# Decay attention with a routed MLP: the scores of two heads as one fp32 product each, straight from the raw rows

## The chip, the cores and the metric

The kernel runs on one core of one Trainium2 chip. The core has TensorE (PE, matrix products and transposes into PSUM), VectorE (DVE), ScalarE (ACT), GpSimd (POOL), SyncE (SP, which here only issues DMAs) and 16 DMA engines. The metric is the device time of one execution in microseconds.

## The reference

```python
# q, k, v: (8, 8, 576, 64); f: (8, 8, 576); w1: 512 x 1024, w2: 1024 x 512, capacity 128
scores = matmul(q, k.T) / sqrt(64)
cum = cumsum(log(clip(f, 1e-4, 1)))
scores = where(causal, -1e9, scores + cum[:, None] - cum[None, :])
attn = exp(scores - max(scores)); attn /= sum(attn) + 1e-9
x = matmul(attn, v)                      # all heads side by side: 576 x 512 per batch
score = x @ w_gate                       # per token
top = the 128 tokens with the largest score
y = relu(x[top] @ w1) @ w2
out = x; out[top] = x[top] + sigmoid(score[top]) * y
```

## The kernel before

The 64 heads are taken as 32 pairs, the two heads of a pair on the two halves of the 128 partitions (64 values of a head each). Of the 576 positions, the first 64 (R) make a short block and the rest four blocks of 128.

For a pair, `pair_ops` loads the raw rows of k (tile `rk`, two DMAs) and of q (tile `rq`, four DMAs into the block layout, with zeros where the short block's product of both heads needs them). Then it splits each into a rounded high part and the rest: `kh`, `qh` by a copy in the type fp32r (L469, POOL), `kl`, `ql` by a subtraction (L476, POOL, for the first 14 pairs also DVE). It also loads, for each head, the row of decays `e` broadcast to all partitions (L500), and has POOL cut it into masked pieces `m` (L370 `affine_select`).

`pair_parts` then makes the scores in six units (rows i, columns k0 to k1): five units of 192 to 448 columns with one product per head on each half of the rows of PE, and one full-height unit of 64 columns for the short block of both heads (`units`, L515 on). Each unit is three products in fp32r, high by high, high by low and low by high (`sc`, L587), two records each for the two heads. DVE adds the decay and takes the minimum (L611, a custom operation that reads the scores in PSUM and `e` or `m`), ACT takes the exponential with a sum (L671), PE transposes the result (`tp`, L691 to L701), ACT or DVE copies it out (`pt`, L308 or L312), PE multiplies by v (`av`, L765; fp32, the two heads on the two halves of the columns of PE), and the result is transposed back (`tb`, L821) and divided by the sums (L827). Per batch a gate is summed (POOL L842, DVE L846), tokens are ranked and the 128 best gathered, and the MLP runs on PE in three fp32r products per tile (L1109 to L1170) with weights that `weight_part` splits during the first half of the run (high L901, low L904).

What is issued in what order is worked out beforehand in Python by the class `Flow`: each piece of work is added with a cost per engine that may take it, what it waits for, a place and the slots (buffers) that it takes and gives back. `Flow.run` goes through a model of the engines' clocks and issues the work in that order; each engine keeps this order. Buffers: two raw k tiles, two raw q tiles, a ring of two for the rounded tiles, two `e`, two `m` per head parity, one tile `x` for half a batch's outputs, eight PSUM banks. `GAP` is the planner's time for a switch of PE from one kind of work to another.

Of the kernel before, what the change touches and what calls it, by code (L numbers as in the profile page):

```python
# [8 lines left out]
F32 = mybir.dt.float32  # L9
# [8 lines left out]
P = 128  # L18
# [12 lines left out]
class Flow:  # L31
# [7 lines left out]

    LAG = {"pe": 0.2, "act": 0.17, "dve": 0.12, "pool": 0.17, "sp": 0.05}  # L40
# [5 lines left out]
           ("turn", "long"): -0.08, ("turn", "short"): -0.08,  # L46
# [41 lines left out]
    def run(self, issued):  # L88
        left = self.todo
        while left:  # L90
# [22 lines left out]
            self.clock[e] = s + t["cost"][e]  # L113
# [22 lines left out]
def kernel(  # L136
# [33 lines left out]
    BD = 0.511  # L170
    WP = 17
    WQ = 3
    R0 = 1.186
    X0 = -3.065
    XE_ = -16.604
    XH_ = 4.193
    XM_ = -24.434
    XB_ = 3.482
    XN_ = -3.264
    XO_ = -0.662  # L180
    XU_ = 0.399
    XQ_ = -1.504
    XR_ = 4.546
    XG_ = 4.106
    PL4 = 42.349
    GW = 175.03
    EPS = 0.011
    LOOK = 13
    HELP1 = 0
    HELP2 = 14  # L190
    SPLIT = 14
    PR = -23.786
    PL = -11.67
    PS = -11.252
    PV = -37.418
    PM = -4.974
    PE_ = 22.794
    PC = -5.754
    PB = 8.281
    PD = 14.978  # L200
    VO = -3.496
    VD = 1
    GD = 0.1
    WS = 29.806
    WD = 12.682
    WL = -15.905
    RK = 30.632
    RD = 8.583
    XP = 0.323
    GO = 12.534  # L210
    GS = 1.969
    GL = 8.861
# [3 lines left out]
    SP = -18.988  # L216
# [10 lines left out]
    def bank(nm):  # L227
# [12 lines left out]
    RING = 2  # L240
# [9 lines left out]
    es = [const.tile([P, S], F32, name=f"e{r}") for r in range(2)]  # L250
    ms = [const.tile([P, 2 * FR + 320 + 448], F32, name=f"m{r}") for r in range(2)]
# [41 lines left out]
    def row(n, k=1):  # L293

        return {"pe": k * max(n * 0.0004375 + 0.0105, 0.108)}
# [18 lines left out]
    flow = Flow({"ps": 8, "raw": 2, "rq": 2, "v": 3, "p0": 4, "p1": 4, "p4": 2, "pt": 2, "ot": 2,  # L314
                 "x": 1, "nm": 10, "h": 1, "hth": 1, "htl": 1, "xth": 1, "xtl": 1, "xe": 2, "srow": 1,
# [120 lines left out]
    raws, ops, used = {}, {}, {}  # L436
# [3 lines left out]
    def pair_ops(p):  # L440
        pl = 9 * p - PL
        r = p % RING
        qh, ql, kh, kl = (ts[r] for ts in (qhs, qls, khs, kls))
        old = used.get(p - RING, [])
        tk = {"q": Token("rq", 2), "k": Token("raw", 2)}
# [9 lines left out]
        def t_q(e):  # L455

            t = raws["q", p] = rqs[p % 2]
# [8 lines left out]
        def hi(dst, nm):  # L466
            def fn(e):
                if e == "pool":
                    nc.gpsimd.tensor_scalar(dst, raws[nm, p], 1.0, 0.0, ALU.mult, ALU.add)  # L469
                else:  # L470
                    copy_on(e, dst, raws[nm, p])
            return fn

        def lo(dst, hi_, nm):
            def fn(e):
                (nc.vector if e == "dve" else nc.gpsimd).tensor_tensor(dst, raws[nm, p], hi_.bitcast(F32), ALU.subtract)  # L476
            return fn

        c1 = {"pool": 0.64}
        c2 = {"pool": 1.46}  # L480
        if p < HELP1:
            c1 = {"pool": 0.64, "act": 0.55, "dve": 0.68}
        if p < HELP2:
            c2 = {"pool": 1.46, "dve": 1.15}
        pl = 9 * p - PS
# [5 lines left out]
        used[p] = []  # L491

        for hh in range(2):
            h = 2 * p + hh
            e_, m_ = es[h % 2], ms[h % 2]
            olde, oldm = decused.get(("e", h - 2), []), decused.get(("m", h - 2), [])
# [42 lines left out]
    def pair_parts(p):  # L539
# [21 lines left out]
        for u, (i, k0, k1) in enumerate(units):  # L561
# [20 lines left out]
            def sc(e, ls, rs, first, last, u=u, i=i, k0=k0, k1=k1):  # L582
                r = p % RING
                for hh in range(2 if i < NF else 1):
                    rows = slice(hh * D, hh * D + D) if i < NF else slice(0, P)
                    o = st["sc", u][hh][:, 0:k1 - k0]
                    nc.tensor.matmul(o, q_rows(ls[r], rows, i), rs[r][rows, k0:k1], start=first, stop=last)  # L587
# [30 lines left out]
            c = row(n)["pe"] if i < NF else pr(n)["pe"]  # L618
            kd = "row" if i < NF else "short"
            if p < SPLIT:  # L620
# [3 lines left out]
            else:  # L624
                x2 = add({"pe": 3 * c}, lambda e, s0=s0, s1=s1, s2=s2: (s0(e), s1(e), s2(e)),
                         after=ops[p][0] + ops[p][1] + ahead, place=place, take=tk_b + tk_n, kind=kd)
            scored[i] = x2
            used[p].append(x2)
            for hh in range(2 if i < NF else 1):
                h = 2 * p + hh  # L630
                def e_(n_, h=h):
                    return lambda: es[h % 2][:, 0:n_]

                def m_(a, b_, h=h, i=i):
                    o_ = {0: 0, 1: 2 * FR, 2: 2 * FR + 320}[i]
                    return lambda: ms[h % 2][:, o_ + a:o_ + b_]

                def m3(h=h):
                    f_ = ms[h % 2][:, FR + P:FR + P + 1]
                    return bass.AP(f_.tensor, f_.offset, [f_.ap[0], [-R, 3], [1, R]])  # L640
# [241 lines left out]
    def weight_part(n):  # L882
# [20 lines left out]
        x2 = add({**({"dve": w / 500 + 0.1} if n < WP else {}), **({"pool": w / 424 + 0.08} if n >= WQ else {})},  # L903
# [355 lines left out]
```

## Time and profile before

| | us |
|---|---|
| median of 3 runs | 448.5 |
| lowest and highest run | 446.15, 450.13 |
| the profiled execution, its own time | 451.17 |
| its span, first to last instruction | 449.4 |

| engine | busy us | share of the span |
|---|---|---|
| PE | 425.1 | 95% |
| DVE | 346.5 | 77% |
| ACT | 338.0 | 75% |
| POOL | 334.9 | 75% |

How to read the rows: L587 is line 587 of the kernel. A name such as sc<-kh,qh is the tile that is written and those that are read. A PE record's busy time reaches from its start until its result is out; records that follow each other overlap, so the time that one costs is the distance from its start to the next start. An fp32 product stands in the profile as two records, an fp32r product and a transpose as one. "x33" counts records. "Idle before <- " is the time for which the engine had nothing in hand before the group, and what ended it. PEclk is the granted clock of PE, as a share of 2.4 GHz.

### The profile page before, as it was taken

To read this page: it belongs to the slowest core of one execution; us is meant where nothing else is said; L and a number is where in the kernel's file an instruction comes from. 1 tells how busy PE (TensorE), PEld (TensorE's weight loads), DVE (VectorE), ACT (ScalarE), POOL (GpSimd) and SP (SyncE) were. 2 spreads that over 40 slices of the span, in tenths; PEclk is the share of its full clock that TensorE was granted. 3 is DMA by queue.
4 is the path that set the end of the run, shared out by engine and by line. 5 is a ranking of instruction groups with operands and counts; after the bars stand their busy time and mean duration, and the time that the engine had idled before them with its cause. 6 is when DMAs were issued, how large, how long until landed. Compare 5 with 4: busy or idle time off the path is not lost. (4 is left out here: it accounts for less than half of the span.)

```text
span 449.4 us, 11669 instructions
## 1 busy us (share of the span) xinstructions
PE 425.1 (95%) x3329; PEld 325.2 (72%) x3329; DVE 346.5 (77%) x1514; ACT 338.0 (75%) x1091; POOL 334.9 (75%) x511
## 2 busy tenths in 40 slices
PE   2999996999989999999999999999999999999995
PEld 1677766686858677868678686868686877878784
DVE  5478988789998689878968987779949995967531
ACT  3479995799988899988789896979987797913221
POOL 7879997799798889987969688689839794142100
PEclk9999996999998999999999999999999999999999
DMA  6566784667766757475554626465546432121010
GB/s 156 155 196 212 195 254 126 195 165 223 195 202 177 217 144 204 118 206 164 187 157 144 202 85 193 159 174 183 159 131 184 135 107 81 54 77 48 23 48 23
DMA packets 73286, 68.07 MB, mean 151 GB/s; under 512 B 25700, under 2 KB 57479, under 8 KB 73223
## 3 DMA queue, kind: packets, MB, share of 16 engines
q1 hardware_dynamic: 71862, 62.99, 47.9%
q0 software_dynamic: 1280, 4.20, 2.8%
q8 instruction: 27, 0.44, 0.4%
q14 instruction: 37, 0.30, 0.3%
q10 hardware_dynamic: 80, 0.15, 0.1%
HBM read 55.59 MB, written 11.70 MB: 150 GB/s over the span
## 5 line engine op out<-in xcount | busy, mean ns | idle before, releaser
L671 ACT ACTIVATE p<-p,nm 128x192 f32<-128x192 f32 (+4 forms) x288 | 166.4, 582 | 19.1 <-DVE nm L611 18.6
L308 ACT COPY pt<-tp 64x128 f32<-64x128 f32 (+4 forms) x386 | 123.9, 365 | 21.0 <-PE tp L696 12.5
L370 POOL TENSOR_SCALAR_AFFINE_SELECT m<-e 128x320 f32<-128x320 f32 (+3 forms) x256 | 111.9, 463 | 25.7 <-DMA e<-eq 15.7
L696 PE MATMUL tp<-ident,p 128*128 128x128 f32 x640 | 112.2, 290 | 6.5 <-DVE nm L611 4.3
L611 DVE CUSTOM_DVE_ANT_0 p<-sc,m 128x320 f32<-128x320 f32 (+3 forms) x224 | 90.0, 429 | 19.4 <-PE sc L587 14.8
L696 PEld LDWEIGHTS tp<-ident,p 128*128 128x128 f32 x640 | 79.2, 147 | 26.5 <-DVE nm L611 6.3
L765 PE MATMUL av<-pt,v 128*64 128x448 f32 (+4 forms) x768 | 91.1, 391 | 0.8 <-DVE nm L611 0.8
L765 PEld LDWEIGHTS av<-pt,v 128*64 128x64 f32 x768 | 45.6, 137 | 42.2 <-issue 29.1
L842 POOL TENSOR_TENSOR gj<-x,wg 128x512 f32<-128x512 f32 x64 | 56.0, 887 | 24.6 <-DVE x L827 20.1
L587 PE MATMUL sc<-kh,qh 64*128 64x192 f32 (+4 forms) x352 | 71.6, 356 | 2.8 <-DVE nm L611 1.7
L587 PE MATMUL sc<-kl,qh 64*128 64x192 f32 (+4 forms) x352 | 64.5, 319 | 0.0
L587 PE MATMUL sc<-kh,ql 64*128 64x192 f32 (+4 forms) x352 | 63.2, 315 | 0.5 <-DVE ql L476 0.5
L587 PEld LDWEIGHTS sc<-kh,qh 64*128 64x128 f32 (+1 forms) x352 | 40.7, 192 | 20.6 <-issue 5.5
L671 ACT ACTIVATION_READ_ACCUMULATOR p<-p,nm 128x1 f32 x288 | 55.2, 192 | 0.0
L476 POOL TENSOR_TENSOR kl<-rk,kh 128x576 fp32r<-128x576 f32 x32 | 46.6, 1456 | 0.2
L611 DVE CUSTOM_DVE_ANT_0 p<-sc,e 128x384 f32<-128x384 f32 x64 | 33.9, 553 | 14.3 <-PE sc L587 12.9
L993 DVE TENSOR_SCALAR_CACHE_REDUCE j<-srow,sg 128x384 uint8<-128x384 f32 (+6 forms) x72 | 41.0, 570 | 1.6
L587 PEld LDWEIGHTS sc<-kh,ql 64*128 64x128 f32 (+1 forms) x352 | 40.6, 194 | 1.1 <-DVE ql L476 0.7
L587 PEld LDWEIGHTS sc<-kl,qh 64*128 64x128 f32 (+1 forms) x352 | 40.0, 194 | 1.0 <-issue 0.5
L476 POOL TENSOR_TENSOR ql<-rq,qh 128x640 fp32r<-128x640 f32 x25 | 38.9, 1554 | 0.2
L308 ACT COPY ot<-av 128x128 f32<-128x128 f32 (+1 forms) x62 | 21.8, 399 | 22.4 <-PE av L765 18.6
L1181 POOL DMA_INDIRECT out_dram<-xe,idx x8 | 8.2, 1031 | 35.8 <-DVE xe L1177 23.2
(108 smaller groups left out, 754.3 us busy)
## 6 DMA issues: line engine op xcount, KB each, us to landing
e<-eq SPq DMA_DIRECT2D x62, 288.0 KB
rq<-in_qk_dram SPq DMA_DIRECT2D x64, 128.0 KB
out_dram<-x SPq DMA_DIRECT2D x16, 512.0 KB
rk<-in_qk_dram SPq DMA_DIRECT2D x32, 192.0 KB
v<-in_v_dram SPq DMA_DIRECT2D x32, 192.0 KB
rk<-in_qk_dram SPq DMA_DIRECT2D x32, 96.0 KB
srow<-sd SPq DMA_DIRECT2D x7, 320.0 KB
v<-in_v_dram SPq DMA_DIRECT2D x32, 64.0 KB
```

Of the source, the lines that this page charges most:

```text
L308: nc.scalar.copy(d, s_)
L370: nc.gpsimd.affine_select(out=dst, in_=src, pattern=w, compare_op=ALU.is_ge, fill=NEG, base=base, channel_multiplier=1)
L476: (nc.vector if e == "dve" else nc.gpsimd).tensor_tensor(dst, raws[nm, p], hi_.bitcast(F32), ALU.subtract)
L587: nc.tensor.matmul(o, q_rows(ls[r], rows, i), rs[r][rows, k0:k1], start=first, stop=last)
L611: nc.vector.tensor_tensor_reduce(out=part(hh, i)[:, x0 - o:x1 - o], in0=b_[:, x0 - k0:x1 - k0], in1=in1(), scale=-0.125, scalar=BIG if fir ...
L671: nc.scalar.activation(x, x, AF.Exp, bias=st["nm", hh, i], scale=-1.0, accum_out=l)
L696: nc.tensor.transpose(tp[:, pos:pos + P], t_[:, o:o + P], ident)
L765: nc.tensor.matmul(avb[p, g][par * D:(par + 1) * D, qo + q0 - g * SPL:qo + q1 - g * SPL], vt[:, j, par * D:(par + 1) * D], pt[:, off:off + ...
L842: nc.gpsimd.tensor_tensor(out=gj[0:n, c0:c1, :], in0=xhs[key][0:n, c0:c1, w0:w1], in1=wg[0:n, hb * HB + w0:hb * HB + w1].unsqueeze(1).broa ...
L993: nc.vector.tensor_scalar(junk[0:n, 0:w, :], src, sg()[0:n, c:c + 1], None, op, ALU.add, accum_out=cnt[0:n, k, c:c + 1])
L1181: nc.gpsimd.indirect_dma_start(out=outs[b][:, :], out_offset=bass.IndirectOffsetOnAxis(ap=q["idx"][0:nr, 0:1], axis=0), in_=q["xe"][0:nr, ...
```

## The change

The scores are one fp32 product per head and unit, directly from the raw tiles `rq` and `rk`. The tiles of the rounded and low parts and the copies and subtractions that fill them go. Raw k, raw q, `e` and `m` get a third tile, `x` a second one. A raw tile is given back by the last of the pair's six score units instead of by the subtraction. The planner's cost for a score unit becomes four passes per column at 2400 columns per us plus 0.03, PE's costs count double before 22 us, some switch times change, and about 50 place constants take new values. The weights' low parts are now open to POOL for all tiles.

```diff
+    HALF = 22.0
-           ("turn", "long"): -0.08, ("turn", "short"): -0.08,
+           ("turn", "long"): 0.01, ("turn", "short"): 0.02, ("long", "turn"): 0.02, ("short", "turn"): 0.02,
...
-            self.clock[e] = s + t["cost"][e]
+            self.clock[e] = s + t["cost"][e] * (2 if e == "pe" and s < self.HALF else 1)
...
-    WQ = 3
+    WQ = 0
...
-    rawp = ctx.enter_context(tc.tile_pool(name="rawp", bufs=2))
+    rawp = ctx.enter_context(tc.tile_pool(name="rawp", bufs=3))
...
-    qhs, qls, khs, kls = ([const.tile([P, w], F32R, name=f"{nm}_{r}") for r in range(RING)]
-                          for nm, w in (("qh", QW), ("ql", QW), ("kh", S), ("kl", S)))
-    rqs = [const.tile([P, QW], F32, name=f"rq{r}") for r in range(2)]
-    es = [const.tile([P, S], F32, name=f"e{r}") for r in range(2)]
-    ms = [const.tile([P, 2 * FR + 320 + 448], F32, name=f"m{r}") for r in range(2)]
+    RQ = 3
+    rqs = [const.tile([P, QW], F32, name=f"rq{r}") for r in range(RQ)]
+    es = [const.tile([P, S], F32, name=f"e{r}") for r in range(3)]
+    ms = [const.tile([P, 2 * FR + 320 + 448], F32, name=f"m{r}") for r in range(3)]
...
-    def row(n, k=1):
-        return {"pe": k * max(n * 0.0004375 + 0.0105, 0.108)}
+    def row(n):
+        return {"pe": n * 4 / 2400 + 0.03}
...
-        tk = {"q": Token("rq", 2), "k": Token("raw", 2)}
+        tk = tks[p] = {"q": Token("rq", 6), "k": Token("raw", 6)}
...
-        a0 = add(c1, hi(kh, "k"), after=[lk] + old, place=pl, give=[tk["k"]])
-        a1 = add(c1, hi(qh, "q"), after=[lq] + old, place=pl + 0.01, give=[tk["q"]])
-        a2 = add(c2, lo(kl, kh, "k"), after=[a0] + old, place=pl + 0.02, give=[tk["k"]])
-        a3 = add(c2, lo(ql, qh, "q"), after=[a1] + old, place=pl + 0.03, give=[tk["q"]])
-        ops[p] = ([a0, a1], [a2, a3])
+        ops[p] = [lk, lq]
...
-            def s1(e, sc=sc):
-                sc(e, qhs, khs, True, False)
-            def s2(e, sc=sc):
-                sc(e, qhs, kls, False, False)
-                sc(e, qls, khs, False, True)
+                    nc.tensor.matmul(st["sc", u][hh][:, 0:k1 - k0], q_rows(raws["q", p], rows, i), raws["k", p][rows, k0:k1],
+                                     start=True, stop=True)
...
-                x1 = add({"pe": c}, lambda e, s0=s0, s1=s1: (s0(e), s1(e)), after=ops[p][0] + ahead, place=place,
-                         take=tk_b + tk_n, kind=kd)
-                x2 = add({"pe": 2 * c}, s2, after=ops[p][1] + [x1], place=place + 0.05, kind=kd)
+            x2 = add(row(n) if i < NF else {"pe": 0.23}, lambda e, s0=s0, sc=sc: (s0(e), sc(e)), after=ops[p] + ahead, place=place,
+                     take=tk_b + tk_n, give=list(tks[p].values()), kind="row" if i < NF else "short")
...
-                xhs[key] = work.tile([P, NCH, HB], F32, tag="x", name=f"x{b}_{hb}", bufs=1)
+                xhs[key] = work.tile([P, NCH, HB], F32, tag="x", name=f"x{b}_{hb}", bufs=2)
```

## Rows read from the trace of the kernel before

**Rows 1.** Busy time of each engine (records in brackets) in four stretches.
```profile
0.00:28.60 28.60, 20.08 (x87) 15.18 (x87) 14.68 (x58) 13.09 (x32) 22.78 (x58) 1.00 0.58 158
28.60:160.94 132.34, 123.00 (x1057) 93.31 (x1056) 112.19 (x462) 115.85 (x391) 117.97 (x173) 0.96 0.68 198
160.94:379.00 218.06, 216.87 (x1799) 166.66 (x1798) 178.91 (x844) 185.50 (x607) 178.95 (x264) 1.00 0.53 156
379.00:449.40 70.40, 65.11 (x394) 50.06 (x390) 40.67 (x152) 23.52 (x61) 15.18 (x18) 0.99 0.13 47
```

Columns of rows 1: the stretch and its length; PE, PE's weight loads, DVE, ACT, POOL; PEclk; DMA share; GB/s.

**Rows 2.** The same view for tiles tp, tb, sc, av alone; PE first.
```profile
28.60:160.94 132.34, 45.68 (x305) 36.16 (x304) 5.79 (x15) 44.57 (x144) 0.96 0.68 198
...
28.60:160.94 132.34, 7.86 (x55) 5.98 (x55) 9.36 (x20) 0.96 0.68 198
...
28.60:160.94 132.34, 44.86 (x402) 35.11 (x402) 58.90 (x159) 0.96 0.68 198
...
28.60:160.94 132.34, 34.41 (x288) 17.01 (x288) 0.61 (x1) 7.83 (x23) 0.96 0.68 198
```

**Rows 3.** Timeline of PE, a pair's scores: start us, us, line, operation.
```profile
334.73 0.28 PE L587 MATMUL sc<-kh,qh 128*128 128x64 f32 x1
...
335.16 0.36 PE L587 MATMUL sc<-kh,qh 64*128 64x192 f32 x2
...
337.09 0.36 PE L587 MATMUL sc<-kl,qh 64*128 64x448 f32 x2
337.30 0.37 PE L587 MATMUL sc<-kh,ql 64*128 64x448 f32 x2
337.59 0.44 PE L696 MATMUL tp<-ident,p 128*128 128x128 f32 x2
```

**Rows 4.** Timeline of PE, short windows from 102.3 to 106.3: av, then transposes.
```profile
102.32 0.60 PE L765 MATMUL av<-pt,v 128*64 128x448 f32 x2
...
102.74 0.55 PE L765 MATMUL av<-pt,v 128*64 128x448 f32 x2
...
103.12 0.55 PE L765 MATMUL av<-pt,v 128*64 128x448 f32 x2
...
105.17 0.66 PE L696 MATMUL tp<-ident,p 128*128 128x128 f32 x4
...
106.23 0.28 PE L587 MATMUL sc<-kh,qh 128*128 128x64 f32 x1
```

**Rows 5.** Timeline of PE near 9.5 us: broadcast of the decay rows.
```profile
9.28 0.68 PE L426 MATMUL eb<-ec,ident 64*128 64x288 f32 x1
...
9.76 0.68 PE L426 MATMUL eb<-ec,ident 64*128 64x288 f32 x1
```

**Rows 6.** Instructions of L904 and L476 on DVE: ns min/median/max, starts.
```profile
L904 DVE TENSOR_TENSOR w1l<-wst,w1h x4: 1391/2002/5645, 31.9 to 65.1; 128x1024 fp32r<-128x1024 f32 x4
...
L476 DVE TENSOR_TENSOR ql<-rq,qh x7: 826/1011/3055, 9.4 to 137.2; 128x640 fp32r<-128x640 f32 x7
```

**Rows 7.** Timeline from 65 to 71.3 us, all engines.
```profile
65.12 5.64 DVE L904 TENSOR_TENSOR w1l<-wst,w1h 128x1024 fp32r<-128x1024 f32 x1
...
68.16 1.52 POOL L476 TENSOR_TENSOR ql<-rq,qh 128x640 fp32r<-128x640 f32 x1
...
71.23 0.47 PE L696 MATMUL tp<-ident,p 128*128 128x128 f32 x1 [4.26 <-DVE nm L611]
```

**Rows 8.** Busy time of L476 (DVE, POOL), then L469 (POOL), middle stretch.
```profile
28.60:160.94 132.34, 9.94 (x6) 26.31 (x18) 0.96 0.68 198
...
28.60:160.94 132.34, 16.50 (x24) 0.96 0.68 198
```

**Rows 9.** Timeline from 5 to 9 us, all engines.
```profile
5.42 2.31 POOL L476 TENSOR_TENSOR kl<-rk,kh 128x576 fp32r<-128x576 f32 x1
...
6.57 1.47 DVE L347 TENSOR_SCALAR ec<-cum 64x576 f32<-64x576 f32 x1
...
8.19 4.18 PE L426 MATMUL eb<-ec,ident 64*128 64x288 f32 x8 [8.19 <-DVE ec L347]
```

More of the change, by code (lines that the diff above doesn't have):

```diff
@@ L168 @@
     FR = 3 * R
-    BD = 0.511
+    BD = 0.402
     WP = 17
-    WQ = 3
[L173 to L187, printed above, removed]
-    LOOK = 13
[L189 to L201, printed above, removed]
+    WQ = 0
+    R0 = -5.724
+    X0 = -10.664
+    XE_ = -10.742
+    XH_ = 3.496
+    XM_ = -19.8
+    XB_ = 3.972
+    XN_ = 1.278
+    XO_ = 3.387
+    XU_ = 0.539
+    XQ_ = -2.214
+    XR_ = -3.319
+    XG_ = 2.438
+    PL4 = 32.118
+    GW = 160.126
+    EPS = 0.046
+    LOOK = 13
+    PR = -40.939
+    PL = -8.453
+    PS = 0.384
+    PV = -48.842
+    PM = -3.506
+    PE_ = 18.626
+    PC = -0.649
+    PB = -12.237
+    PD = 13.348
+    VO = 0.39
     VD = 1
     GD = 0.1
[L204 to L212, printed above, removed]
+    WS = 43.054
+    WD = 12.208
+    WL = -11.468
+    RK = 27.538
+    RD = 4.88
+    XP = 1.445
+    GO = 24.739
+    GS = 1.812
+    GL = 16.246
     LG = 2.69
@@ L215 @@
     SX = 2.5
-    SP = -18.988
+    SP = -24.46
     const = ctx.enter_context(tc.tile_pool(name="const", bufs=1))
-    rawp = ctx.enter_context(tc.tile_pool(name="rawp", bufs=2))
+    rawp = ctx.enter_context(tc.tile_pool(name="rawp", bufs=3))
     work = ctx.enter_context(tc.tile_pool(name="work", bufs=2))
@@ L312, in copy_on @@
             nc.vector.tensor_copy(d, s_)
-    flow = Flow({"ps": 8, "raw": 2, "rq": 2, "v": 3, "p0": 4, "p1": 4, "p4": 2, "pt": 2, "ot": 2,
-                 "x": 1, "nm": 10, "h": 1, "hth": 1, "htl": 1, "xth": 1, "xtl": 1, "xe": 2, "srow": 1,
+    flow = Flow({"ps": 8, "raw": 3, "rq": 3, "v": 3, "p0": 4, "p1": 4, "p4": 2, "pt": 2, "ot": 2,
+                 "x": 2, "nm": 10, "h": 1, "hth": 1, "htl": 1, "xth": 1, "xtl": 1, "xe": 2, "srow": 1,
                  "oh": 1, "gs": 2, "dg": 1}, EPS, {"dve": BD}, GW)
@@ L434, in bcast @@
                 for g in range(2)]
-    raws, ops, used = {}, {}, {}
+    raws, ops, tks = {}, {}, {}
     dec = {}
@@ L441, in pair_ops @@
         pl = 9 * p - PL
-        r = p % RING
-        qh, ql, kh, kl = (ts[r] for ts in (qhs, qls, khs, kls))
-        old = used.get(p - RING, [])
-        tk = {"q": Token("rq", 2), "k": Token("raw", 2)}
+        r = p % 2
+        tk = tks[p] = {"q": Token("rq", 6), "k": Token("raw", 6)}
         def t_k(e):
@@ L455, in t_q @@
         def t_q(e):
-            t = raws["q", p] = rqs[p % 2]
+            t = raws["q", p] = rqs[p % RQ]
             nc.sync.dma_start(out=t[0:D, 0:R], in_=qk[2 * p][:, 0, 0:R])
@@ L580, in s0, with sc @@
                         st["pw", hh, i] = pw.tile([P, (640, 896)[i - 2]], F32, tag=f"p{i % 2}", name=f"p{p}_{u}_{hh}", bufs=4)
-            def sc(e, ls, rs, first, last, u=u, i=i, k0=k0, k1=k1):
-                r = p % RING
+            def sc(e, u=u, i=i, k0=k0, k1=k1):
                 for hh in range(2 if i < NF else 1):
                     rows = slice(hh * D, hh * D + D) if i < NF else slice(0, P)
-                    o = st["sc", u][hh][:, 0:k1 - k0]
-                    nc.tensor.matmul(o, q_rows(ls[r], rows, i), rs[r][rows, k0:k1], start=first, stop=last)
-            def s1(e, sc=sc):
-                sc(e, qhs, khs, True, False)
-            def s2(e, sc=sc):
-                sc(e, qhs, kls, False, False)
-                sc(e, qls, khs, False, True)
+                    nc.tensor.matmul(st["sc", u][hh][:, 0:k1 - k0], q_rows(raws["q", p], rows, i), raws["k", p][rows, k0:k1],
+                                     start=True, stop=True)
             def part(hh, i):
@@ L617, in pair_parts @@
                 ahead = ahead + [scored[i + 2 if i < 2 else i]]
-            c = row(n)["pe"] if i < NF else pr(n)["pe"]
-            kd = "row" if i < NF else "short"
-            if p < SPLIT:
-                x1 = add({"pe": c}, lambda e, s0=s0, s1=s1: (s0(e), s1(e)), after=ops[p][0] + ahead, place=place,
-                         take=tk_b + tk_n, kind=kd)
-                x2 = add({"pe": 2 * c}, s2, after=ops[p][1] + [x1], place=place + 0.05, kind=kd)
-            else:
-                x2 = add({"pe": 3 * c}, lambda e, s0=s0, s1=s1, s2=s2: (s0(e), s1(e), s2(e)),
-                         after=ops[p][0] + ops[p][1] + ahead, place=place, take=tk_b + tk_n, kind=kd)
+            x2 = add(row(n) if i < NF else {"pe": 0.23}, lambda e, s0=s0, sc=sc: (s0(e), sc(e)), after=ops[p] + ahead, place=place,
+                     take=tk_b + tk_n, give=list(tks[p].values()), kind="row" if i < NF else "short")
             scored[i] = x2
-            used[p].append(x2)
             for hh in range(2 if i < NF else 1):
@@ L631, in e_ @@
                 def e_(n_, h=h):
-                    return lambda: es[h % 2][:, 0:n_]
+                    return lambda: es[h % 3][:, 0:n_]
                 def m_(a, b_, h=h, i=i):
                     o_ = {0: 0, 1: 2 * FR, 2: 2 * FR + 320}[i]
-                    return lambda: ms[h % 2][:, o_ + a:o_ + b_]
+                    return lambda: ms[h % 3][:, o_ + a:o_ + b_]
                 def m3(h=h):
-                    f_ = ms[h % 2][:, FR + P:FR + P + 1]
+                    f_ = ms[h % 3][:, FR + P:FR + P + 1]
                     return bass.AP(f_.tensor, f_.offset, [f_.ap[0], [-R, 3], [1, R]])
```

26 lines of the change are left out of this document (3 added, 23 removed).

## The prediction

> **What bounds the kernel now.** I read three views in this order. First the busy time by stretch [rows 1]: from 160.94 to 379 us TensorE (PE) is busy 216.87 of 218.06 us, so there the kernel is bound by PE and every microsecond put on PE is a microsecond of time. From 28.6 to 160.94 us PE is busy 123.0 of 132.34, and DVE, ACT and POOL stand at 112, 116 and 118: four engines that nearly balance. Busy is not work done, since overlapping records hide short waits, so I priced that stretch by what its records cost when nothing waits. It holds 305+55 transposes, 402 score records and 288 attention-times-V records [rows 2]. A pair of heads has 33 score records (three products of 5x2 half-height and one full-height unit) and they take 337.59-334.73 = 2.86 us in one run [rows 3]; the 24 av records of a pair take 105.17-102.32 = 2.85 us and ten transposes 106.23-105.17 = 1.06 us [rows 4]. So: 360 x 0.107 = 38.5; 402/33 x 2.86 = 34.8; 288/24 x 2.85 = 34.2; together 107.5 of 132.34 us. About 5 of the missing 25 I give to switches between kinds of work, which are more frequent here (an estimate: some 23 more breaks in the score runs, at 0.2 each); **about 20 us are waits of PE on the other engines**. After 160.94 none of that size is left.
>
> Where the waits come from is the third view. The subtraction of the low part of w1 on DVE takes 1391 ns at its fastest and 5645 at its slowest, the one of q 826 to 3055 [rows 6]. The slow one starts at 65.12 and ends only after POOL has finished its last rounding product at 69.68; DVE's score work stands behind it, and the transpose at 71.23 has PE idle for 4.26 us [rows 7]. In this trace a DVE subtraction of two SBUF operands is held up by POOL's work on SBUF: 5.6 us in place of 1.4.
>
> **The change, part by part.**
>
> *Scores on PE.* Three fp32r products become one fp32 product. That an fp32 product is two records, each streaming its columns twice, I read off two places. The broadcast of the decay, an fp32 product on one row half with 128 weight columns, has starts 9.28 and 9.76: 0.48 us for 288 columns is 2x288 at 1.2 GHz, with the weight load hidden [rows 5] (this early PE runs at the lower level by its spacing, though the clock column reads 1.00 [rows 1]; the spacing decides). The av product, fp32 on the two column halves, has starts in twos, 102.32, 102.74, 103.12: 0.375 us for 448 columns is 2x448 at 2.4 GHz [rows 4]. The code issues both records of one half and then both of the other, yet two start at a time and the shapes never mix, so the halves run beside each other without a stagger. Two heads on row halves in fp32 are shown nowhere: that is the main unknown. The fp32r records of two row halves do start together [rows 3], so I take them as concurrent.
>
> Price of a pair before: half-height units 337.59-335.16 = 2.43, of which some 0.2 is load ahead and drain (last record 0.29 to the next kind, 0.21 inside the run), so 2.23; full-height unit 0.43 [rows 3]. After: 192+384+192+320+448 = 1536 columns x 4 / 2400 = 2.56; full-height unit two weight loads for three, 0.29. Difference +0.33-0.14 = +0.19; if the full-height unit gains nothing, +0.33. I take 0.26 x 32 pairs = **+8.3 us**, range 6 to 11. Fully on the path after 160.94; before that only as far as PE is the bound.
>
> *Rounding removed.* Per pair POOL loses kh, qh, kl and mostly ql. In the middle stretch that is 26.31+16.50 = 42.8 of POOL's 118 us, and DVE loses six ql, 9.94 of 112 us [rows 1, 8]. It costs nothing elsewhere; no added operation replaces it. Of the weights' low parts DVE's stay eligible; with POOL emptier they meet fewer long POOL runs. If w1's four ran at their fastest, the slowest alone would give back 5.6-1.4 = 4.2 us [rows 6]. So DVE falls to about 112-10-3 = 99, ACT stays at 116 unless copies move to DVE (both engines are allowed), mean 107. PE needs 107.5+5+12x0.26 = 115.6. All under 120, so I put the stretch's end about 11 us earlier net, which is 14 of the 20 us of waits recovered against the 3 us of the added PE work already counted: **-14 us**. Ends: 5 if ACT's 116 stays the bound, 20 if all goes.
>
> *Start.* The decay row on DVE starts at 6.57 and takes 1.47 us while POOL's first kl runs from 5.42 to 7.73; PE's first instruction waits for it until 8.19 [rows 9]. Without kl it is up to about 1 us sooner, and the first score unit is whole after one product instead of three spread ones. I take **-2 us**, 0 to -5 (more if PE reaches its higher clock sooner).
>
> *Third tiles, raw loads.* The scores now read the raw rows, so a raw tile comes free with the last of six score units, not after rounding, and the load of pair p+3 waits for it on SP's queue; behind it stand e, v and weight loads, and POOL's masks wait for e. The cover is a third tile: two pairs ahead, 20 us here. I price it at 0 (two more memsets on DVE at the start, under the wait for f); without cover the load's six issues and landing, some 5 us, would fall on PE at each pair. The third e and m tiles let masks run ahead; they gain nothing where PE is bound.
>
> *Places, x twice, planner prices.* Another order of the same work: bounded by the same 20 us of waits, nothing of its own taken.
>
> **Sum** against the profiled span: +8.3-14-2 = -7.7, so 449.4 becomes 441.7. The execution lies 0.9 above the median of the runs (448.5); 448.5-7.7 = 440.8, say **441 us**.
>
> A rule that speaks against this: the Trainium skill (TensorE: Matmul & The Clock Gate, section "Part 3: Packing small matmuls — row/col tiling") says that matmuls start and end strictly in program order. By it the second head's first pass could not start before the first head's second pass, which is rival 1, and the sum would be about 465 instead of 441. The av starts in twos of [rows 4], with both records of one half ahead in the program, don't agree with it on column halves; no row here shows row halves in fp32.
>
> **The rivals.**
> 1. *Stagger.* If the second row half starts one pass late, every run of score units is longer by one record of its last unit, 2x307/2400 = 0.26 us in the mean. At some three runs per pair (estimate, 35 runs for 12 pairs in the middle stretch) that is 93 x 0.26 = 24 us: 465 us. For it: program order. Against: [rows 4]. Chance 0.09.
> 2. *No concurrency on row halves.* 2.56 more per pair, +82: about 523 us. Against: the fp32r halves. Chance 0.03.
> 3. *ACT is the next bound; slower or no change.* ACT's 115.85 us in the middle stretch [rows 1] are not touched. If its exponentials and copies hold the pace, only the direct DVE-POOL blocks vanish, 5 us, with 1 at the start: 448.5+8.3-6 = 451 (446 to 456). It decides from the point where the recovered waits are under 8 us. For it: ACT at 88% of that stretch; against: copies may move to DVE. Chance 0.2.
> 4. *Everything recovered*, 20 us and 5 at the start: 448.5+8.3-25 = 432. Chance 0.13.
>
> **How the numbers follow.** The forecast (436 to 447) has 0.55. One per cent is 4.5 us, about what a measurement of this kernel tells from no change. Faster (below 444): three quarters of the forecast plus rival 4, 0.54. Within 1%: the rest of the forecast and 0.6 of rival 3, 0.26. Slower: 0.4 of rival 3, rivals 1 and 2, 0.20. The range of 8 in 10 reaches over rival 4's centre and through rival 3: 431 to 456.
>
> **What would show it.** The pair of score records starting together with a step of 2n/2400 (448 columns: 0.375 us); a whole run of six units at about 3.05 us; PE idle in 28 to 161 us falling from 9 us to under 3; no DVE subtraction of 5 us; POOL's busy time near 200 us; PE still 99% busy after 160 us. Wrong if record starts alternate by head, if PE after 160 us shows waits on ACT, or if the middle stretch takes as long as before with ACT above 95%.

## The result, and the profile after

The changed kernel takes 431.32 us (median of 4 runs, 430.80 to 432.24) where the kernel before took 448.13 on the same chip: a ratio of 0.963, interval 0.958 to 0.967, so 16.8 us or 3.7% less. The profiled execution of after has a span of 429.0 us and a time of 430.8; its counterpart before spans 449.4.

Times of the runs below are medians; their ratios are to the kernel before, run again beside each group of experiments (448.9 to 450.4 us), and leave out executions in the chip's slower state.

Busy time by stretch, after (columns as in [rows 1]: stretch and length; PE, PE's weight loads, DVE, ACT, POOL; PEclk; DMA share; GB/s):

```profile
0.00:28.60 28.60, 20.74 (x109) 14.38 (x110) 18.33 (x89) 19.13 (x57) 17.79 (x58) 1.00 0.73 209
28.60:160.94 132.34, 131.35 (x1017) 95.08 (x1017) 113.19 (x556) 122.87 (x415) 91.87 (x157) 1.00 0.75 214
160.94:379.00 218.06, 216.65 (x1613) 161.48 (x1611) 173.37 (x806) 169.59 (x561) 93.38 (x174) 1.00 0.49 145
379.00:429.00 50.00, 44.51 (x250) 34.54 (x245) 25.04 (x90) 10.37 (x21) 10.08 (x12) 0.99 0.13 44
```

In the middle stretch PE idles 1 us where it idled 9.3 [rows 1]. POOL has lost a fifth of its time there (118 to 92) and about half later (179 to 93). ACT, at 123 of 132, is busier than before without holding PE up. After 160.94 us nothing seems to happen: 216.65 us busy, 216.87 before. That is misleading. The way to see it is the one that the prediction used for the middle stretch alone: to price each of PE's records at what it costs when nothing waits. What is left of the stretch is called unpriced below.

The same stretches for tiles tp, tb, sc, av, hp and yp alone, after (PE first); the middle stretch, then the late one:

```profile
28.60:160.94 132.34, 40.07 (x313) 34.31 (x311) 7.89 (x28) 42.95 (x140) 1.00 0.75 214
...
28.60:160.94 132.34, 8.90 (x60) 6.23 (x60) 11.20 (x24) 1.00 0.75 214
...
28.60:160.94 132.34, 45.13 (x284) 30.17 (x284) 63.89 (x171) 1.00 0.75 214
...
28.60:160.94 132.34, 36.23 (x310) 18.57 (x312) 0.81 (x3) 7.80 (x21) 1.00 0.75 214
...
28.60:160.94 132.34, 6.26 (x24) 4.28 (x24) 1.18 (x2) 1.00 0.75 214
...
28.60:160.94 132.34, 1.54 (x6) 1.13 (x6) 0.00 (x0) 1.00 0.75 214
...
160.94:379.00 218.06, 57.31 (x450) 50.55 (x450) 9.99 (x33) 63.07 (x201) 1.00 0.49 145
...
160.94:379.00 218.06, 13.27 (x90) 9.41 (x90) 16.67 (x36) 1.00 0.49 145
...
160.94:379.00 218.06, 53.21 (x358) 34.75 (x358) 78.32 (x211) 1.00 0.49 145
...
160.94:379.00 218.06, 49.45 (x424) 25.20 (x422) 0.00 (x0) 12.65 (x36) 1.00 0.49 145
...
160.94:379.00 218.06, 26.95 (x96) 16.64 (x96) 4.77 (x8) 1.00 0.49 145
...
160.94:379.00 218.06, 28.66 (x114) 20.80 (x114) 3.74 (x5) 1.00 0.49 145
```

The prices are the prediction's own: 0.107 us for a transpose, 2.85/24 for an av record, and for the scores one run, 3.106 us for the 22 records of a pair (shown further down; before 2.86 for 33). One price is new, for the experts' products: 20 yp records take 233.94-229.18 = 4.76 us, 0.238 each.

Timeline of PE around such a run of yp, after (start us, us, line, operation):

```profile
229.18 0.48 PE L1115 MATMUL yp<-w2h,hth 128*128 128x512 f32 x1
...
233.94 0.60 PE L718 MATMUL av<-pt,v 128*64 128x448 f32 x2
```

Middle stretch, after: (313+60+12) x 0.107 = 41.2 (the 12, like 52 of the late stretch, are transposes of the experts' tiles, from the same view), 284/22 x 3.106 = 40.1, 310/24 x 2.85 = 36.8, 30 x 0.238 = 7.1; together 125.2 of 132.34, so **7.1 us are unpriced, against 24.8 before**. Late stretch (592 transposes, 358, 424 and 210 records): 63.3+50.5+50.4+50.0 = 214.2 of 218.06, 3.8 unpriced. The same sum for before (586 transposes, 582 score records, 408 of av, 198 of the experts) gives 208.7, so 9.3 us were unpriced there while PE was 99% busy. A few records of a trace can be missing, so a microsecond either way means nothing; the differences, 17.7 and 5.5 us, do.

Not all of the 24.8 were waits. In two places of that stretch PE was granted the lower of its two clock levels.

Busy time by stretch, before, in those two places (PEclk is the third number from the end):

```profile
69.70:76.50 6.80, 5.27 (x25) 5.23 (x26) 5.01 (x20) 4.37 (x14) 4.79 (x10) 0.50 0.49 132
134.50:137.90 3.40, 3.35 (x17) 3.12 (x16) 3.40 (x17) 2.16 (x6) 3.40 (x4) 0.50 0.63 203
```

Transposes start 0.213 us apart there and 0.109 right after. The first fall came within the 4.26 us of idling of [rows 7], the second 1.9 us after PE had resumed (at 132.63) from a wait of 1.5 us. Half of the 5.27 + 3.35 us that PE worked at this level, 4.3 us, is an estimate of what it cost. In the middle stretch of after the clock is 1.00 throughout (before 0.96, [rows 1]). So of the 17.7 us that went, some 4.3 were the clock, which followed on waits, and some 13.4 the waits themselves.

Timeline of PE in short windows from 167.9 to 171.3, after: one pair's scores.

```profile
167.95 3.17 PE L554 MATMUL sc<-rk,rq 128*128 128x64 f32 x22
171.06 0.28 PE L990 MATMUL ip<-tok,oh 128*128 128x1 f16 x5
...
168.22 0.43 PE L554 MATMUL sc<-rk,rq 64*128 64x192 f32 x2
...
168.65 0.81 PE L554 MATMUL sc<-rk,rq 64*128 64x384 f32 x4
...
170.15 0.60 PE L554 MATMUL sc<-rk,rq 64*128 64x448 f32 x2
...
170.53 0.60 PE L554 MATMUL sc<-rk,rq 64*128 64x448 f32 x2
```

Records come in twos, 7 ns apart in the trace (168.216 and 168.223; the rows are rounded), and within the run the next two follow about 2n/2400 later: 170.53-170.15 = 0.38 for 448 columns (0.375 before rounding, 2n/2400 is 0.373). The trace does not name the heads. One product is two records that stream its columns twice each, so a unit of two heads that takes 4n/2400 in all has its heads side by side, and the two records that start together are read as one of each head. The run takes 171.06-167.95 = 3.11 us where the three products took 2.86 [rows 3]; the shortest of the 11 unbroken runs after 28.6 us in this trace takes 3.05.

To compare kernels as wholes, the table below reads when PE had done a given amount of work, in us of work at the same prices for all (a pair's scores count the same in every kernel, so one that takes longer for them falls behind); each row has the time from the start in each trace. Other prices for the small kinds of record move all columns together, by up to 4 us in the last row, and the differences between columns by some 0.3 us.

```
work   before  core_alone  after_displaced_1  after_displaced_2  after   before_displaced_1  before_displaced_2
  10     31.4        27.3               27.3               25.3   25.7                27.2                27.8
  40     64.9        65.9               61.8               61.8   58.0                66.0                73.8
  80    116.4       110.8              106.2              105.8  101.1               114.5               127.6
 120    165.0       154.4              151.0              150.4  145.3               160.0               173.5
 200    249.6       240.9              235.1              235.1  229.5               243.8               257.2
 380    432.9       427.1              419.5              420.8  412.1               433.8               451.8
```

After against before: 5.7 us ahead at 10, 19.8 at 120, 20.8 at 380. So 5.7 us at the start, 14.1 in the middle with the added score work already paid, and 1.0 later, where the score work adds 20 pairs x 0.245 = 4.9 us. (The traces differ by 20.4 us and the medians by 16.8: before's profiled execution lies above the median of its runs.) The columns between are taken up with the experiments.

### The profile page after: what moved, and what is told of

Its sections match the earlier page's. It is cut to its first block, busy times and chain, and to the rows that moved or that the text cites. A ratio compares the mean times of both kernels' runs of the same rounds, so it can differ in the third digit from the quotient of the medians.

```text
span 429.0 us, 10648 instructions
## 1 busy us (share of the span) xinstructions
PE 413.3 (96%) x2977; PEld 305.5 (71%) x2977; DVE 329.9 (77%) x1538; ACT 322.0 (75%) x1053; POOL 213.1 (50%) x399
## 5 line engine op out<-in xcount | busy, mean ns | idle before, releaser
L624 ACT ACTIVATE p<-p,nm 128x448 f32<-128x448 f32 (+4 forms) x288 | 166.0, 580 | 13.3 <-DVE nm L572 12.6
L366 POOL TENSOR_SCALAR_AFFINE_SELECT m<-e 128x320 f32<-128x320 f32 (+3 forms) x256 | 105.6, 439 | 90.1 <-DMA e<-eq 50.4
L554 PE MATMUL sc<-rk,rq 64*128 64x192 f32 (+4 forms) x704 | 110.5, 424 | 2.0 <-DVE nm L572 1.8
L572 DVE CUSTOM_DVE_ANT_0 p<-sc,m 128x384 f32<-128x384 f32 (+3 forms) x224 | 89.6, 428 | 12.0 <-PE sc L554 11.0
L554 PEld LDWEIGHTS sc<-rk,rq 64*128 64x128 f32 (+1 forms) x704 | 72.8, 190 | 22.7 <-ACT pt L304 4.6
L799 DVE TENSOR_REDUCE gu<-gj 128x4 f32<-128x512 f32 x64 | 28.5, 472 | 14.7 <-POOL gj L795 14.7
L780 DVE TENSOR_TENSOR x<-tb,rn 128x512 f32<-128x512 f32 x32 | 22.0, 687 | 22.3 <-PE tb L774 22.2
L572 DVE DVE_READ_ACCUMULATOR2_ANT nm<- 128x1 f32 x416 | 33.8, 81 | 0.0
L572 DVE CUSTOM_DVE_ANT_1 p<-sc,m,nm 128x192 f32<-128x192 f32 x64 | 26.3, 412 | 1.0 <-POOL m L366 0.7
L1062 PE MATMUL hp<-w1h,xth 128*128 128x512 f32 x64 | 26.7, 417 | 0.0
L1115 PE MATMUL yp<-w2h,hth 128*128 128x512 f32 x64 | 26.1, 407 | 0.0
```

The costliest lines, as they stand in the source:

```text
L366: nc.gpsimd.affine_select(out=dst, in_=src, pattern=w, compare_op=ALU.is_ge, fill=NEG, base=base, channel_multiplier=1)
L554: nc.tensor.matmul(st["sc", u][hh][:, 0:k1 - k0], q_rows(raws["q", p], rows, i), raws["k", p][rows, k0:k1], start=True, stop=True)
L572: nc.vector.tensor_tensor_reduce(out=part(hh, i)[:, x0 - o:x1 - o], in0=b_[:, x0 - k0:x1 - k0], in1=in1(), scale=-0.125, scalar=BIG if fir ...
L624: nc.scalar.activation(x, x, AF.Exp, bias=st["nm", hh, i], scale=-1.0, accum_out=l)
L799: nc.vector.tensor_reduce(out=gu[0:n, hp, c0:c1], in_=gj[0:n, c0:c1, :], axis=mybir.AxisListType.X, op=ALU.add)
L1062: nc.tensor.matmul(q["hp", n][0:nr, :], q["xth"][:, c, 0:nr], r_[:, c, cs], start=(c == 0 and k_ == 0), stop=False)
```

## The experiments

### The fp32 product alone

The product, raw operands and no rounding; everything else as before: two raw, e and m tiles, one x, the old places and planner prices.

```
-    HALF, new GAP, new places, "raw": 3, "rq": 3, es/ms of 3, x of 2
+    old GAP, old places,       "raw": 2, "rq": 2, es/ms of 2, x of 1
```

> The fp32 product from the raw rows without rounding, and nothing else: two tiles for raw rows, decay and masks, one for x, the old places and the old switch times of the planner. Theory A (the gain is the rounding taken off POOL and DVE, so their waits in the first 160 us go): 431 to 436 us. Theory B (the gain is the new order of the work, the places): 443 to 452 us, since the added PE time of some 8 us stands against the few waits that go by themselves.

Measured: 445.13 us, 0.987 of before (0.981 to 0.993). In the table it is 4.1 us ahead of before at 10, 10.6 at 120, 5.8 at 380: it wins early and loses 4.8 us after, the added score work to a few tenths. PE's idle time in the middle fell from 9.3 to 3.7 us, and no wait of the sort in [rows 7] is left there (the longest is 1.6 us). The three subtractions of w1's low part that stayed on DVE take 1.2 us each, where the kernel before has 1.4 to 5.6 [rows 6].

Busy time by stretch, core_alone:

```profile
28.60:160.94 132.34, 128.60 (x966) 86.32 (x966) 106.68 (x510) 120.10 (x406) 86.08 (x151) 0.99 0.71 207
160.94:379.00 218.06, 217.60 (x1594) 154.31 (x1591) 171.82 (x810) 182.38 (x587) 93.90 (x178) 1.00 0.50 149
```

Instructions of w1l on DVE, core_alone (ns min/median/max, first and last start):

```profile
L857 DVE TENSOR_TENSOR w1l<-wst,w1h x3: 1172/1206/1226, 30.4 to 42.5; 128x1024 fp32r<-128x1024 f32 x3
```

The time is theory B's, but not its reason alone: the waits did go, as theory A has it, and the core is worth 5.8 us by the ratio, near the prediction's 7.7. It stops 11 us short of the changed kernel (0.987 against 0.963 of 448).

### Rounding put back

The changed kernel, with the rounding instructions on POOL and DVE again; their result goes into a tile that nothing reads, and a raw tile waits for them too. There is one such tile, so the roundings of all pairs run one behind the other, which the kernel before, with its ring of two, does not require.

```
+        a0 = add(c1, hi(rr[:, 0:S], "k"), after=[lk] + rold[-1:], place=pr_, give=[tk["k"]])
+        a2 = add(c2, lo(rr[:, 0:S], rr[:, 0:S], "k"), after=[a0], ...)
+        ... the same two for q
```

> The changed kernel, with the four rounding operations of each pair still done (into a tile that nobody reads; POOL, and DVE may take the subtractions of the first 14 pairs as before). Theory A: 442 to 449 us, with waits of PE on DVE between 30 and 160 us back to 15 us or more. Theory B: under 436 us.

Measured: 457.94 us, 1.016 of before (1.011 to 1.021), 24 us above after by the ratios and slower than either theory had it. Instructions of the added subtraction on DVE (ns min/median/max, first and last start):

```profile
L468 DVE TENSOR_TENSOR rr<-rq,rr x5: 826/1157/2964, 20.0 to 126.5; 128x640 fp32r<-128x640 f32 x5
L468 DVE TENSOR_TENSOR rr<-rk,rr x4: 760/1506/2051, 37.0 to 142.1; 128x576 fp32r<-128x576 f32 x4
```

Waits of PE, the same kernel, whole run (us in total, times, longest):

```profile
PE sc L570 <- DVE nm L588: 3.8, 3, 2.1
PE sc L570 <- DVE pt L309: 3.1, 1, 3.1
PE tp L665 <- DVE nm L588: 3.1, 3, 1.9
```

The stretched subtractions come back, 826 to 2964 ns, and so do PE's waits on DVE, though in the middle stretch they come to some 6 us and not to the 15 expected; most of the loss is again in gaps that PE's busy time hides. Priced as above, 20.4 us are unpriced in the middle stretch and 15.7 in the late one (after: 7.1 and 3.8). With rounding kept, time is lost after 160.94 us too. Up to some 7 of the 24 us may be the order of the work, which the edit upsets (displacements, below), and what the single tile costs is not told apart.

### The start

Transposes of the identity on PE ahead of its first work: 24 in the kernel before, 40 in the changed one.

```
+        for n_ in range(24):   # 40
+            nc.tensor.transpose(w_[:, 0:P], ident, ident)
```

> The kernel before with 24 transposes of the identity put on PE before its first product, where it stands idle until 8.2 us. Theory C (about 5 us of the gain is PE's higher clock, which comes at about 15 us instead of 28): the spacing of transposes halves before 20 us and the time falls by 4 to 6 us, to 442 to 444. If the clock is not what the start costs, under 1 us of change.

> The changed kernel with 40 transposes of the identity ahead of PE's first product, so that PE works from about 1.4 us on without a break. Theory C (the low clock at the start is on the path here): products of the decay and the first scores at the 2.4 GHz spacing from about 5 us, 2 to 4 us faster, 427.5 to 429.5. Theory C': the early gain is lost again to waits for DVE and ACT, as in the kernel before, under 1 us.

Measured: 451.0 us, 1.001 (0.996 to 1.006), and 431.35 us, 0.958 (0.953 to 0.963; after itself 0.958 to 0.967). Neither moves the time, as the second half of each expectation has it. In the first, the spacing of PE's records goes to its 2.4 GHz value at about 4.6 us; the trace is 2.4 us ahead at 10 us of work and 0.1 at 30. In the second, 1.3 ahead at 1 us of work and nothing at 40. A lead of PE in the first 25 us was taken back by waits on the other engines (in the first trace the longest is 4.9 us on DVE's nm, in the second 2.2).

### Places and tiles, one without the other

Four kernels between the two: the new places in the kernel before; the old places in the changed kernel; and core_alone with only the third tiles and x twice, or only with the new places and prices.

```
before_new_places:     old product and tiles        new places
new_tiles_old_places:  new product, third tiles     old places, new prices
core_third_tiles:      new product, third tiles     old places, old prices
core_new_places:       new product, two tiles       new places, new prices
```

> The kernel before with the place constants of the changed one (rounding placed where its raw loads are). Theory A: 446 to 452 us, as before. Theory B: 436 to 441 us.

> The changed kernel with the old place constants: the third tiles, the second x and the planner's new prices stay. Core alone took 445.1 and the full change 431.3, so 13.8 us are to be divided. Theory D (the order is what gives them, by longer unbroken runs of one kind of work on PE): 441 to 446 us. Theory E (the tiles give them, by letting loads and masks run ahead): 431 to 435 us.

> Core alone (fp32 product, no rounding, old places, old planner prices) with the third tiles and the second x. Theory D: 443 to 446 us. Theory E: 431 to 436 us.

> The changed kernel with the old counts of tiles (two raw, two e, two m, one x); places and planner prices are the new ones. Theory D: 431 to 436 us. Theory E: 441 us or more, with PE waiting for scores whose masks or raw rows come late.

Measured: 461.63 us, 1.025 (1.017 to 1.031) for the new places in the kernel before; 440.92, 0.981 (0.975 to 0.986), for the old places in the changed kernel; 443.30, 0.987 (0.979 to 0.994), with the tiles alone; 443.09, 0.985 (0.979 to 0.990), with the places alone. Each adds nothing that can be measured to core_alone's 0.987, and both together bring 0.963. Neither theory's fast case came: D asked for 431 to 436 from the places alone, E from the tiles alone. The new places in the kernel before were outside both of its theories. That looks as if the places needed the tiles. The next runs take that reading apart.

### One kind of tile taken away

```
after_two_raw:    "raw": 2, "rq": 2
after_two_masks:  es, ms for r in range(2)
after_one_x:      "x": 1
```

> The changed kernel with two tiles for raw q and raw k in place of three; e, m and x as changed, and the changed places. Theory P (the new places need all the tiles they were worked out for): taking any of them away gives back 5 us or more, here 437 to 444. Theory Q (one kind of tile carries the gain, and it is the raw one, since a raw tile now comes free only with the last score unit): 440 to 444 here, and 430 to 433 for the two kernels with the other tiles taken away. Theory R (masks running ahead carry it): 430 to 433 here.

> The changed kernel with two tiles for e and two for m in place of three; raw tiles and x as changed, and the changed places. Theory P: 437 to 444. Theory Q (raw tile): 430 to 433. Theory R (the masks on POOL, which may run one pair further ahead, carry the gain): 440 to 444, with PE waiting on DVE's nm and POOL's m between 28 and 161 us.

> The changed kernel with one tile for x in place of two. Theory P in its strict form (any tile): 435 or more. Theories Q and R: 430 to 433, as x belongs to the expert part after the middle stretch.

Measured: 439.89 us, 0.979 (0.975 to 0.984); 449.42, 1.001 (0.996 to 1.005); 438.40, 0.976 (0.972 to 0.980). By the ratios every kind of tile costs 6 us or more (the masks' 17, beyond theory P's 444), even x, of which the middle stretch has little use. With two masks PE waits again:

Waits of PE, after_two_masks:

```profile
PE av L718 <- DVE nm L572: 5.6, 5, 2.3
PE tp L649 <- DVE nm L572: 3.9, 3, 3.0
```

That would settle it for "the places need all the tiles", were there not a second explanation: any difference sets the planner on another order, and any other order costs as much.

### The places displaced, all tiles kept

33 place constants, each displaced by up to 0.5 either way (a pair of heads is 9 on that scale), two sets of displacements, in both kernels. (The diff of the change gives 37 constants new values, not about 50; these are the 37 without BD, WQ, GW and EPS.) Of the first set in the kernel before:

```
-    R0 = 1.186          +    R0 = 1.138
-    X0 = -3.065         +    X0 = -3.005
-    XE_ = -16.604       +    XE_ = -16.180
```

> The changed kernel with all its tiles; 33 place constants are each displaced by up to 0.5 either way (a pair of heads is 9 on this scale), the same computation. Theory T (the places are fitted to one schedule, and the last 7 us of the gain are that fit, not the tiles): 435 to 441, as much as one x tile or the raw tiles cost. Theory U (tile counts and the rough order carry it): within 2 us of the changed kernel, 429 to 433.

> The changed kernel with another set of displacements of up to 0.5. Theory T: 435 to 441. Theory U: 429 to 433.

> The kernel before with its 33 place constants displaced by up to 0.5. Theory T: 453 to 460, since its order was fitted as closely; then core_alone's 445, on places fitted to other work, compares with about 456 and not with 448, and the core change alone is worth some 11 us. Theory U: 446 to 451.

> The kernel before with another set of displacements of up to 0.5. Theory T: 453 to 460. Theory U: 446 to 451.

Measured: 437.95 us, 0.975 (0.968 to 0.983), and 439.11, 0.978 (0.970 to 0.986), for the changed kernel, as theory T has it; 452.63, 1.007 (1.003 to 1.012), and 469.14, 1.042 (1.032 to 1.052), for the kernel before, either side of T's 453 to 460.

Waits of PE, before_displaced_2:

```profile
PE tp L696 <- DVE nm L611: 8.5, 5, 4.8
...
PE av L765 <- DVE nm L611: 5.1, 3, 4.3
PE sc L587 <- DVE nm L611: 4.3, 8, 1.4
```

A shift that changes no computation costs the changed kernel 5.6 to 6.8 us of its 16.8 (by the ratios, 0.0126 and 0.0151 of 448), and the kernel before 3 to 19. So the two kernels compared are each the best of the three that were run, and a small sample says that neighbours are slower. Part of the cost is the clock again: in the middle stretch of before_displaced_2 it is 0.94. What the x tile and the raw tiles seemed to be worth (0.976 and 0.979) is what a displacement costs (0.975 and 0.978); only the masks' tile, at 1.001, stands out from it. The ratios of these kernels side by side:

```
                              with the rounding            without
places fitted to the kernel   1 (before)                   0.963 (after)
other places or tiles         1.007, 1.025, 1.042          0.975, 0.976, 0.978, 0.979, 0.981,
                              1.016 (rounding put back)    0.985, 0.987, 0.987; 1.001 (two masks)
```

Every unfitted order without rounding lies below every one with it, two masks by less than the intervals; the kernel of the next section, with rounding, adds 1.051. Between displaced neighbours the change is worth 0.975 to 0.978 against 1.007 to 1.042, 13 to 30 us in the four pairings.

### DVE relieved of the subtractions

The kernel before with every low part computed on POOL.

```
-    HELP2 = 14      WP = 17     WQ = 3
+    HELP2 = 0       WP = 0      WQ = 0
```

> The kernel before with every subtraction of a low part on POOL (none may go to DVE). If the waits of PE in 28.6 to 160.94 us come from DVE subtractions held up by POOL (5645 ns in place of 1391), they go with them: 440 to 446. If they come from the sheer amount of rounding work, POOL, busy 118 of 132 us there, gets some 9 us (six ql at 1.46) and the four w1l more, becomes the bound of that stretch, and the kernel is slower: 455 to 465. About 449 if both hold and cancel.

Measured: 471.30 us, 1.051 (1.045 to 1.057).

Busy time by stretch, before_no_dve_subtraction:

```profile
28.60:160.94 132.34, 119.92 (x984) 85.45 (x984) 87.40 (x441) 116.14 (x378) 117.56 (x166) 0.99 0.61 181
```

Its longest waits of PE in that stretch, and the one on POOL, which falls before 28.6 us:

```profile
PE tp L696 <- ACT ot L308: 4.0, 4, 1.2
PE tp L696 <- ACT p L671: 2.4, 4, 1.3
...
PE sc L587 <- POOL ql L476: 2.4, 1, 2.4
```

DVE falls from 112 to 87 us in the middle stretch, and none of its rounding subtractions can be held up any more. Yet the kernel is 23 us slower: more than either displacement cost, and above both ranges of the expectation. For the meetings of DVE and POOL to be the whole of the loss, as the first theory has it (440 to 446), the new order alone would have to cost 25 to 31 us, where displacements cost 3 to 19. before_displaced_1 points the same way: its slowest w1l takes 2.3 us, not 5.6, and it is no faster than before. So the meetings were one way in which the rounding cost time, and not the main one. That the amount of rounding is the rest fits after_rounding_kept, but is not shown here: POOL's busy time in the middle stretch stays at 118 of 132 us, and of PE's waits there 9 of 12 us are on ACT and none on POOL.

The Trainium skill (SBUF — State Buffer, section "🔬 SBUF: two separate sides") says that a DVE operation with two SBUF inputs and a GpSimd operation that reads SBUF exclude each other for a whole instruction. The stretched subtractions agree with it, 1391 to 5645 ns [rows 6] and 826 to 2964 above, and so do the 1172 to 1226 ns without rounding; but the slowest lasts through five POOL instructions one behind the other, from 65.12 to past 69.68, not one. By that rule alone this kernel should have gained, and it lost 23 us.

## Why the prediction came out as it did

**Where the sum went wrong.** The sum was +8.3 for the scores, -14 for the waits and -2 at the start, -7.7 in all. Read from the two traces it is +7.8 for the scores, -17.7 in the middle stretch, -5.7 at the start and -5.5 after 160.94 us, which had no term: -21.1, where the traces differ by 20.4 and the medians by 16.8. So the 431.3 us lie below the forecast's 436 to 447. The step behind most of this is that the order of the work was put at nothing of its own; it and the others follow one by one. (The sum's "0.9 above the median" sets the span of the profiled execution against a time of a run; the execution's own time, 451.17, lies 2.7 above.)

*Scores on PE, +8.3.* Right in mechanism and size. A pair's run takes 3.106 us, expected 3.05; +0.245 a pair or 7.8 us in all. Two fp32 products on row halves run beside each other, without a stagger: rivals 1 and 2 are out. The Trainium skill's rule of strict program order (TensorE: Matmul & The Clock Gate, section "Part 3: Packing small matmuls — row/col tiling") does not hold in the reading that made it rival 1: with the records read as above, the second head's first record starts 7 ns after the first head's (168.223 and 168.216) and 0.26 us ahead of the first head's second one (168.483). Whether the two records of a product stand in the program one behind the other, as that reading needs, no trace here shows; from product to product the starts keep the program's order.

*Waits, -14.* Right in mechanism. By the prediction's own pricing the middle stretch had 24.8 us that were not work; it expected 10.8 to be left, and 7.1 are. The step that failed here is "about 20 us are waits of PE on the other engines": some 4.3 of them were PE at its lower clock, which the 0.96 in [rows 1] showed and the sum left out. Without these, 13.4 us went, near the 14. On places fitted to another kernel the size was about right or too large: 15.7 are left in core_alone, 12.4 and 13.2 in the displaced ones (the same sums, with their records).

*After 160.94 us, no term.* Here a step failed: "After 160.94 none of that size is left", and with it "every microsecond put on PE is a microsecond of time". It was read off a busy share of 99%, though the same paragraph says that busy is not work done. Priced, the late stretch had 9.3 us of its own; 5.5 went, and paid for the 4.9 us of scores added there, so the added work made the stretch no longer. With rounding put back 15.7 are unpriced in it, and a displacement of the kernel before leaves 10.5 to 16.1. PE counts as busy while short gaps disappear under overlapping records.

*Start, -2.* The cause was right for a part: the decay is read on DVE at 6.18 in place of 6.57, takes 0.45 us in place of 1.47 [rows 9], and PE starts at 6.78 in place of 8.19.

Timeline from 5 to 9 us, after, all engines:

```profile
6.18 0.45 DVE L343 TENSOR_SCALAR ec<-cum 64x576 f32<-64x576 f32 x1
...
6.78 2.74 PE L422 MATMUL eb<-ec,ident 64*128 64x288 f32 x5 [6.78 <-DVE ec L343]
```

The size was not: 5.7 us at 10 us of work, of which 1.4 are the earlier start; the rest is, by this reading, mostly the clock, whose higher level PE reaches at about 15 us and not at 28.6 (last section). But this is not a gain of the change: both displaced versions of before have the higher level by 17.8 us (transposes 0.109 us apart). Nor can the lead be added up as the prediction did. The kernels with warmed PE lost theirs, and the displaced versions of before, with nothing of the change in them, were 4.2 and 3.6 us ahead at 10 us of work and behind at 40. How much of the 5.7 lasts is open.

*Third tiles, raw loads, 0.* The cover was not needed: core_alone has two raw tiles, each given back only by the last score unit, and none of the 5 us per pair that the prediction set for a lack of cover appears. For x and raw, nothing told apart from a displacement. For the masks the price of 0 may be wrong, since without their third tile the changed kernel is 17 us slower; a kernel with two masks and places fitted to it was not tried, so this stays open.

*Places, 0.* This is the term that was mis-sized most: "Another order of the same work: bounded by the same 20 us of waits, nothing of its own taken." An order is worth 6 us and more in this kernel, as the displaced ones show, and not only in the middle stretch: at 120 us of work they are 5 to 6 us behind after, at 380 us 7 to 9. With a displaced order the changed kernel takes 438 to 439 us, inside the prediction's own range of 436 to 447; as it stands it takes 431. The prediction did not ask whether the new constants suit the new work better than their neighbours do, and gave that no price. That accounts for 6 to 7 of the 9 us (by the medians) by which the forecast was off; the rest is not told apart from the terms above.

*The rivals.* Rival 3 (ACT next) is out: ACT is at 93% of the middle stretch and PE at 99%. Rival 4, at 0.13, came closest: its 20 us in the middle and 5 at the start were 17.7 and 5.7. What it lacked is the 5.5 us after 160.94; that its 432 is nearly the median all the same is luck, since the profiled execution of before lies 3 us above the median of its runs.

*What would show it.* The score step, the run's length, idle PE under 3 us, no DVE subtraction of 5 us and PE at 99% after 160 us all came as said; POOL's busy time is 213 us, expected near 200. One came in another way than meant: in after all twelve subtractions of the weights' low parts run on POOL (2.36 us for each of w1), so DVE has none that could be held up. In core_alone three of w1 stayed on DVE and ran unhindered, as the prediction meant.

## What to carry over

Price what an engine does, record by record, in every stretch before calling it bound: at 99% busy this PE still had 9 us that were not work. Read the granted clock before you call the rest waits: 4 of 25 us here were the lower level. In a kernel whose order is worked out by constants, displace the constants a little before you read anything into an edit: here that alone costs 3 to 19 us, as much as most of the edits. The core of this change, tried on the old places and tiles, looked worth a third of the whole (0.987 against 0.963). Work taken off an engine that feeds the bound one (POOL here, 335 to 213 us) can repay more than it adds to the bound one.

## What was not expected of the hardware

*The clock at the start.* PE's spacing shows the lower level at first in both kernels while the clock column reads 1.00. The traces explain it: their clock records begin at 15.06 us in after and at 28.71 in before, just where the spacing changes, and ahead of the first record the view shows 1.00. In after the step changes within the first pair's scores:

Timeline of PE in short windows from 12.3 to 16.6 us, after:

```profile
13.58 0.74 PE L554 MATMUL sc<-rk,rq 64*128 64x320 f32 x2
...
14.12 1.28 PE L554 MATMUL sc<-rk,rq 64*128 64x320 f32 x4
...
15.77 0.65 PE L554 MATMUL sc<-rk,rq 64*128 64x192 f32 x4
```

Records of 320 columns start 14.12-13.58 = 0.54 us apart (0.534 before rounding), 640 columns at 1.2 GHz; in the 192-column records from 15.6 on the step is 0.16 (15.608 to 15.770), 384 at 2.4. PE had worked without a long pause since 6.78 us. In before the same change comes at about 28.6 us: transposes at 28.05 and 28.26 are still 0.213 apart. PE's work had been broken up there by short waits, of which the timeline shows one at 22.00 us. Displaced, the same kernel reaches the higher level at 16 to 17 us, so the late rise belongs to that order. With the 24 transposes ahead it came at 4.6 us, fell back by 8.2, after PE had idled from 5.8, and was back before 22.5; in that trace there are records of the clock by then, and the column does show it:

Busy time by stretch, before_warm_pe:

```profile
0.00:28.60 28.60, 24.22 (x131) 18.41 (x133) 15.98 (x67) 15.26 (x40) 23.42 (x59) 0.76 0.55 156
```

At the start of a trace the spacing of records is the safer reading of the two.
